# The opening of a fused attention and MLP kernel: triangles added by TensorE, v loaded whole by SyncE, quad 1 normalised in two parts, weight columns with stride two

## The chip, the cores and the metric

The kernel runs on one core of a Trainium2 chip. A core has a matmul engine (TensorE, PE in the profile; its weight loads are shown as PEld), VectorE (DVE), ScalarE (ACT), GpSimd (POOL) and SyncE (SP), each with its own queue of instructions, which it works through in order. They share the on-chip memory SBUF; matmuls write to PSUM, of which this kernel uses all eight banks. Loads and stores are issued by POOL (which can convert fp32 to bf16 on the way) and by SyncE, and are carried out by 16 DMA engines. The metric is the device time of one execution in microseconds; less is better. The profile's times count from the start of its span.

## The reference, cut to what matters

For 8 batches of 8 heads, 576 positions and 64 dimensions, a causal attention with a forget gate; its output, with the heads laid side by side to 512 columns, goes through a two-layer MLP with a tanh-approximated gelu and 2048 hidden columns.

```python
scores = scale * np.matmul(q, k.transpose(0, 1, 3, 2))
cum = np.cumsum(np.log(np.clip(f, 0.0001, 1.0)), axis=-1)
decay = cum[:, :, :, None] - cum[:, :, None, :]
scores = np.where(causal, -1000000000.0, scores + decay)
attn = np.exp(scores - np.max(scores, axis=-1, keepdims=True))
attn = attn / (np.sum(attn, axis=-1, keepdims=True) + 1e-09)
x = np.matmul(attn, v)            # then (batch, position, head * 64)
out = gelu_tanh(x @ w_in) @ w_out
```

The decay between a query and a key is a factor of the query times a factor of the key. The query's factor cancels in the division, so the kernel multiplies v, and the ones under the denominator, by the key's factor `wT`, and needs no decay on the scores.

## The kernel before

**Units of work.** Four heads of one batch are a quad; there are 16. A quad's scores are made with keys on the partitions and queries along the free axis, in three rounds (`rounds`): keys 0 to 127 against queries 0 to 511, then the last 64 queries of that strip with keys 128 to 255, then keys 256 to 511. The last 64 keys meet the last 64 queries in a corner of round 0 that would be masked anyway. In each round PE writes two pairs of PSUM banks (two heads each), ScalarE takes the exponential of each pair into `pt`, and POOL (`mask`, L182) writes zeros where the key is later than the query, with one `affine_select` per diagonal block, two for the first strip.

**From pt to xT.** `product` multiplies `pt` with a weight column. With `w_bf` it gives the denominators (`denominators`), with the weighted v, `vw`, the numerators, 32 dimensions of each head at a time (`out_groups(i, y)`). `reciprocals` transposes the denominators on VectorE (L220), inverts them (L222) and spreads them again (L224); `normalise` (L229) multiplies the numerators into `xT`, which is the MLP's input with the model dimension on the partitions. `make_vw` (L136) makes vw of a quad with two multiplies of 128x640 and two of 64x128 elements, the even and the odd dimensions of each head apart; it runs on VectorE for quads 0 and 1 and on POOL for the others.

**MLP.** `mlp_mm` (L241) multiplies 128 columns of w_in, the stationary operand, with 288 columns of xT; sixteen such column tiles make the hidden layer, each followed by a gelu on ScalarE (L250). `mlp_out` (L273) makes the output tiles from w_out, VectorE copies them out of PSUM (L278) and SyncE stores them. It is a generator: `pull` takes some of its matmuls at a time to fill PE's time between the attention rounds of the next quads.

**Order.** The order on each engine is the order in which the program writes it (`tc.manual_schedule()`). `startup` is the opening: it loads f, q and k of quads 0 and 1, v of batch 0 and the first half of w_in, makes the key factors, the transposed q and k (L125) and the vw of quads 0 and 1, and then interleaves the score rounds of both quads with their products. Some matmuls on a blank tile (`warm_up`, L297) are put in between. The rest of w_in (L115), q and k of quad 2, w_out (L119), q and k of quad 3 and v of batch 1 are loaded by POOL, between the masks. The main loop then runs, for batch 0, the hidden layer, `step(2)`, `step(3, 2)`, `step(4, 3)`: a step makes the scores of one quad and the products of the quad before it, in three rounds with fills. In these steps `make_vw(2)` stands in round 1 of its step and `make_vw(3)` and all later ones in round 0, between masks.

**Tiles.** Two bank pairs, tag "s", take turns for scores and hidden layer; one pair each has the tags "po" and "x". A product that is written to a pair waits until VectorE has read what stood there.

Of the kernel before, what the change touches and what calls it, by code (L numbers as in the profile page):

```python
# [16 lines left out]
def kernel(  # L17
# [67 lines left out]
    blank = singles.tile([128, 512], BF16, name="blank")  # L85
    pools = {"s": psS, "po": psO}
# [23 lines left out]
    w_out_hbm = moe_w_out.rearrange("(t p) n -> p t n", p=128)  # L110

    def load_w_in(c):
        n = slice(D_FF // 2 * c, D_FF // 2 * (c + 1))
        for u in range(QPB):
            nc.gpsimd.dma_start(out=w_in_sb[:, 2 * u:2 * u + 2, n], in_=w_in_hbm[u, :, :, n])  # L115

    def load_w_out(c):
        n = N_FT // 4
        return nc.gpsimd.dma_start(out=w_out_sb[:, n * c:n * (c + 1), :],  # L119
                            in_=w_out_hbm[:, n * c:n * (c + 1), :])  # L120
# [11 lines left out]
    def make_vw(i, eng=nc.gpsimd):  # L132
        h0 = 4 * (i % QPB)
        for p, n, slot in ((128, NT, 0), (64, 1, HEAD)):
            for y in range(2):
                eng.tensor_mul(  # L136
                    vw[i % 2][:p, slot:slot + n, :, 32 * y:32 * y + 32],
                    v_nat[(i // QPB) % 2][:p, 0:n, h0:h0 + 4, y::2],
                    wT[:p, i, 0:n, :].unsqueeze(3).to_broadcast([p, n, 4, D // 2]))
# [4 lines left out]
    def score_round(i, r, tags=("s", "s")):  # L144
# [19 lines left out]
        else:  # L164
            c0 = 0
            for (t, q0, nq) in parts:
                for c in range(2):
                    block(c, 0, 128, 128 * t, q0, nq, c0, c0 == 0)
                c0 += nq
        for g in range(2):  # L170
            nc.scalar.activation(p[:, 2 * g:2 * g + 2, off:off + n],  # L171
                                 tiles[g][:, :, 0:n], AF.Exp, scale=scale)

    def mask(i, r):
        p = pt[i % 2]
        for (t, q0, nq) in rounds[r][1]:
            if q0 == 128 * t:
                o = strip_off[t]
                within = [[0, 4], [1, 128]]
                for p0, p1, pattern in ([(0, 64, within), (64, 128, [[0, 4], [0, 2], [1, 64]])]  # L180
                                        if t == 0 else [(0, 128, within)]):
                    nc.gpsimd.affine_select(  # L182
                        out=p[p0:p1, :, o:o + 128], in_=p[p0:p1, :, o:o + 128],
                        compare_op=ALU.is_ge, fill=0.0, base=0, pattern=pattern,
# [33 lines left out]
    def reciprocals(i, po):  # L218
        den = den_pool.tile([128, S], FP32, name="den", tag="den")
        nc.vector.transpose(out=den, in_=po)  # L220
        rec = den_pool.tile([128, S // 32], FP32, name="rec", tag="rec")
        nc.vector.reciprocal(rec, den[:, 0:S:32])  # L222
        rb = den_pool.tile([128, S], FP32, name="rb", tag="rb")
        nc.vector.transpose(out=rb.rearrange("p (c j) -> p c j", j=32),  # L224
                            in_=rec.unsqueeze(2).to_broadcast([128, S // 32, 32]))
        rbs[i] = rb

    def normalise(i, y, po):
        nc.vector.tensor_mul(xT[i // QPB % 2][:, 2 * (i % QPB) + y, :], po, rbs[i])  # L229
# [7 lines left out]
    def mlp_mm(b, ft, ph, dts):  # L237
        hS = S // 2
        for dt in dts:
            for j in range(2):  # L240
                nc.tensor.matmul(  # L241
                    ph[:, j, 0:hS],
                    w_in_sb[:, dt, 128 * ft:128 * ft + 128],
# [55 lines left out]
    def startup():  # L299
        nc.sync.dma_start(out=f_sb, in_=f.rearrange("b h s -> (b h) s"))  # L300
        load_qk(0)
        make_identity(nc, ident_f32)
        load_qk(1)
        load_v(0, nc.gpsimd, slice(0, 4))
        load_v(0, nc.gpsimd, slice(4, 8))
        load_w_in(0)
# [27 lines left out]
        make_vw(1, nc.vector)  # L334

        for r, tags in enumerate((("s", "s"), ("x", "s"), ("s", "x"))):
            score_round(0, r, tags)
            warm_up(warm, 5)
            mask(0, r)
            if r == 0:  # L340
                load_w_in(1)
        score_round(1, 0)
        warm_up(warm, 5)
        score_round(1, 1, ("x", "s"))
        denominators(0)
        mask(1, 0)
        score_round(1, 2, ("s", "x"))
        attn_out(0, 0)
        mask(1, 1)
        load_qk(2)  # L350
        attn_out(0, 1, "s")
        mask(1, 2)
# [123 lines left out]
```

## Time and profile before

| | |
|---|---|
| median of 3 runs | 348.53 us (348.51 to 349.12) |
| the profiled execution, as a run | 348.87 us |
| its span | 347.2 us |
| PE busy | 334.9 us, 96% |
| ScalarE, VectorE, POOL busy | 198.4, 124.6, 131.5 us |
| matmuls of the hidden layer (L241) | 1024, 128.5 us |
| matmuls of the output layer (L273) | 1908, 134.6 us |
| POOL's selects (L182) | 80, 51.8 us |
| POOL's share of vw (L136) | 56 multiplies, 44.9 us |

A row of the timeline reads: start in us, duration in us, engine, line, operation, output and inputs, shape, how many instructions are merged into the row, and in brackets how long the engine stood idle before it and what ended that. A row by stretches gives the stretch, its length, and the busy time of PE, PEld, DVE, ACT and POOL, then the granted clock of TensorE, the busy share of the DMA engines and GB/s. A row of the DMA view gives a queue, its packets, MB and its share of 16 engines; q0 is POOL's queue, q1 SyncE's. A row of a group gives its busy time and the mean duration of one in ns, then the idle time before it.

### The profile page before, as it was taken

The page shows a single profiled execution, that of the slowest core. Times are in us where ns is not written, and L with a number is a line of the kernel's source. Part 1 is how long each engine was busy: PE and PEld are TensorE (multiplying, and loading weights), DVE is VectorE, ACT ScalarE, POOL GpSimd, SP SyncE. Part 2 cuts the span into 40 slices and gives each one's busy share as a digit, 9 for nine tenths or more (in the row PEclk, how much of TensorE's full clock was granted, in tenths as well). Part 3 has the DMA queues.
Part 4 walks back from the last instruction along what each step waited for, and adds up shares of the span by engine and source line. Part 5 has one row for each costly group of instructions (what it writes and reads, how often), then busy time and mean ns, then how long its engine had stood idle before and what let it go on. Part 6 is the DMA issues. An engine that isn't in the chain of part 4 may idle for free.

```text
span 347.2 us, 11023 instructions
## 1 busy us (share of the span) xinstructions
PE 334.9 (96%) x5022; PEld 197.6 (57%) x5022; DVE 124.6 (36%) x169; ACT 198.4 (57%) x244; POOL 131.5 (38%) x197
## 2 busy tenths in 40 slices
PE   7968999999999999999999999999999999999995
PEld 2336744477444774467554674457644675557642
DVE  7776034652342504433234413325133312430011
ACT  4853677676745567566655567566754566516400
POOL 8795339754162232716143241725035500200000
PEclk9989999999999999999999999999999999999999
DMA  7999998559311590019310391119201100010021
GB/s 127 202 180 207 220 188 198 98 89 229 61 62 64 112 192 32 34 59 206 70 65 35 102 203 31 37 60 186 50 34 63 51 14 2 35 62 30 2 89 63
DMA packets 42063, 33.37 MB, mean 96 GB/s; under 512 B 29600, under 2 KB 31648, under 8 KB 42016
## 3 DMA queue, kind: packets, MB, share of 16 engines
q0 software_dynamic: 8624, 15.99, 25.9%
q1 hardware_dynamic: 33392, 16.67, 17.3%
q8 instruction: 39, 0.64, 0.8%
q14 instruction: 8, 0.07, 0.1%
HBM read 36.85 MB, written 9.44 MB: 133 GB/s over the span
## 4 chain that ended last, share of the span: by engine, by line
PE 87%; ACT 5%; issue 2%; DMA 2%; POOL 2%; DVE 2%; ACTq 0%; DVEq 0%; POOLq 0%
PE ps_h L241 36%; PE pso L273 32%; PE po L198 10%; PE ps_s L151 8%; ACT pt L171 5%; DMA q_c<-in_q_dram 2%; POOL pt L182 1%; DVE den L220 0%; POOL w_in_sb L115 0%; DVE qT L125 0%; DVE rb L224 0%; DVE xT L229 0%; DVE o_st L278 0%; ACT gT L250 0%; POOL k_c L96 0%
## 5 line engine op out<-in xcount | busy, mean ns | idle before, releaser
L273 PE MATMUL pso<-w_out_sb,gT 128*32 128x512 bf16 (+1 forms) x1908 | 134.6, 379 | 0.0
L241 PE MATMUL ps_h<-xT,w_in_sb 128*128 128x288 bf16 x1024 | 128.5, 286 | 1.4 <-DVE xT L229 0.9
L171 ACT ACTIVATE pt<-ps_s 128x1024 bf16<-128x1024 f32 x96 | 92.6, 1024 | 51.7 <-PE ps_s L151 51.6
L250 ACT ACTIVATE gT<-ps_h 128x576 bf16<-128x576 f32 x128 | 82.5, 651 | 67.0 <-PE ps_h L241 67.0
L241 PEld LDWEIGHTS <-w_in_sb 128*128 128x128 bf16 x1024 | 99.5, 98 | 31.2 <-issue 5.1
L182 POOL TENSOR_SCALAR_AFFINE_SELECT pt<-pt 128x512 bf16<-128x512 bf16 (+1 forms) x80 | 51.8, 658 | 123.8 <-ACT pt L171 122.3
L273 PEld LDWEIGHTS <-gT 128*32 128x32 bf16 (+1 forms) x1908 | 59.0, 97 | 53.4 <-issue 0.8
L278 DVE COPY o_st<-pso 128x512 f32<-128x512 f32 x36 | 24.7, 685 | 71.0 <-PE pso L273 70.9
L136 POOL TENSOR_TENSOR vw<-v_nat,wT 128x640 bf16<-128x640 f32 (+1 forms) x56 | 44.9, 830 | 0.2
L220 DVE STREAM_TRANSPOSE den<-po 128x576 f32<-128x576 f32 x16 | 12.5, 783 | 83.8 <-PE po L198 83.8
L229 DVE TENSOR_TENSOR xT<-po,rb 128x576 bf16<-128x576 f32 x32 | 24.1, 757 | 46.3 <-PE po L198 46.1
L151 PE MATMUL ps_s<-qT,kT 32*64 32x64 bf16 (+6 forms) x896 | 35.9, 292 | 1.9 <-DVE qT L125 1.0
L151 PEld LDWEIGHTS <-kT 32*128 32x128 bf16 (+1 forms) x896 | 15.1, 97 | 27.4 <-issue 23.9
L198 PE MATMUL po<-pt,vw 128*32 128x64 bf16 (+4 forms) x768 | 28.8, 287 | 0.3 <-DVE den L220 0.3
L125 DVE STREAM_TRANSPOSE kT<-k_c 128x576 f32<-128x576 f32 x16 | 20.0, 1247 | 12.1 <-DMA k_c<-in_k_dram 12.1
L198 PEld LDWEIGHTS <-vw 128*32 128x32 bf16 x768 | 13.9, 99 | 14.8 <-issue 8.6
L96 POOL DMA_DIRECT2D k_c<-in_k_dram x16 | 9.2, 573 | 29.6 <-DVE kT L125 25.3
L125 DVE STREAM_TRANSPOSE qT<-q_c 128x576 f32<-128x576 f32 x16 | 19.9, 1243 | 1.1 <-DMA q_c<-in_q_dram 0.9
L198 PE MATMUL po<-pt,w_bf 128*32 128x512 bf16 (+5 forms) x384 | 15.2, 284 | 2.8 <-POOL pt L182 2.8
L102 POOL DMA_DIRECT2D v_nat<-in_v_dram x15 | 11.5, 775 | 8.2 <-DMA w_out_sb<-in_moe_w_out_dram 5.0
L224 DVE STREAM_TRANSPOSE rb<-rec 128x576 f32<-128x576 f32 x16 | 12.5, 778 | 0.5
L198 PEld LDWEIGHTS <-w_bf 128*1 128x1 bf16 (+1 forms) x384 | 6.5, 89 | 10.6 <-issue 6.1
(32 smaller groups left out, 69.2 us busy)
## 6 DMA issues: line engine op xcount, KB each, us to landing
out_dram<-o_st SPq DMA_DIRECT2D x36, 256.0 KB, 2.0
v_nat<-in_v_dram SPq DMA_DIRECT2D x24, 256.0 KB, 6.4
k_c<-in_k_dram POOLq DMA_DIRECT2D x16, 288.0 KB, 6.2
q_c<-in_q_dram POOLq DMA_DIRECT2D x16, 288.0 KB, 7.1
w_in_sb<-in_moe_w_in_dram POOLq DMA_DIRECT2D x4, 512.0 KB, 9.8
w_out_sb<-in_moe_w_out_dram POOLq DMA_DIRECT2D x4, 512.0 KB, 11.8
v_nat<-in_v_dram POOLq DMA_DIRECT2D x9, 128.0 KB, 7.3
v_nat<-in_v_dram POOLq DMA_DIRECT2D x4, 256.0 KB, 14.7
```

What stands on the lines that cost most here:

```text
L125: nc.vector.transpose(out=dst[i % 2].rearrange("p s c -> p (s c)").bitcast(FP32) .rearrange("p (t a) -> p a t", a=S // 32), in_=src[i % 2] ...
L136: eng.tensor_mul(vw[i % 2][:p, slot:slot + n, :, 32 * y:32 * y + 32], v_nat[(i // QPB) % 2][:p, 0:n, h0:h0 + 4, y::2], wT[:p, i, 0:n, :].u ...
L151: nc.tensor.matmul(tiles[h // 2][m0:m0 + m, h % 2, c0:c0 + nq], kk[32 * h:32 * h + 32, k0:k0 + m, c], qq[32 * h:32 * h + 32, q0:q0 + nq, c ...
L171: nc.scalar.activation(p[:, 2 * g:2 * g + 2, off:off + n], tiles[g][:, :, 0:n], AF.Exp, scale=scale)
L182: nc.gpsimd.affine_select(out=p[p0:p1, :, o:o + 128], in_=p[p0:p1, :, o:o + 128], compare_op=ALU.is_ge, fill=0.0, base=0, pattern=pattern, ...
L198: nc.tensor.matmul(po[r0:r0 + w.shape[-1], o:o + nq], w, p[:, h, col:col + nq], start=(n < 2), stop=(n in (0, len(product_parts) - 1)), sk ...
L220: nc.vector.transpose(out=den, in_=po)
L229: nc.vector.tensor_mul(xT[i // QPB % 2][:, 2 * (i % QPB) + y, :], po, rbs[i])
L241: nc.tensor.matmul(ph[:, j, 0:hS], w_in_sb[:, dt, 128 * ft:128 * ft + 128], xT[b % 2][:, dt, hS * j:hS * (j + 1)], start=(dt == 0), stop=( ...
L250: nc.scalar.activation(gT[:, ft, o:o + S].rearrange("p (j n) -> p j n", j=2), ph[:, :, 0:hS], AF.Gelu_apprx_tanh)
L273: nc.tensor.matmul(ps[m:m + w, :], gT[:, ft, c + m:c + m + w], w_out_sb[:, ft, :], start=(ft == 0), stop=(ft == N_FT - 1), skip_group_chec ...
L278: nc.vector.tensor_copy(st, ps)
```

## The change

**Masks of quads 0 and 1.** Two 128x128 tiles `lows` hold 0 where a key may be seen and -32768 elsewhere, one for the first strip with its folded corner and one for the other diagonal blocks. POOL makes them and a bf16 identity at the start. `score_round(..., masked=True)` adds the right one to each diagonal block of the scores with a matmul against the identity, so that the exponential gives zero; that is 16 matmuls of 128 columns for a quad. POOL's selects for these two quads are gone. Four of the groups of five warm-up matmuls become groups of four.

**Loads.** v of batch 0 is issued by SyncE in five whole tiles (eight heads), behind a wait for q of quad 0. The first load of w_in waits for the third of them. All of w_in, q and k of quad 2, w_out, q and k of quad 3, and v of batch 1 for its first four heads are issued by POOL one after the other; v of batch 1 for the other four heads is issued by SyncE once q of quad 3 is there. v of batch 2 is issued in step 2, after round 2.

**Quad 1.** `reciprocals` and `normalise` take a range of queries. After the products of the first four parts the queries 0 to 255 are complete; they are divided and written to xT, and the other 320 follow.

**Columns with stride two.** `make_vw` writes vw with the dimensions in order, in one multiply of 128x1280 and one of 64x256, and the product picks the even or odd ones with a stride of two. Likewise a hidden tile takes every second column of 256 columns of w_in, so that two neighbouring rows of w_out lie on one partition and are loaded as one run.

**Steps 2 and 3.** `make_vw(2)` and `make_vw(3)` move to the end of round 2 of their step, behind the last mask.

```diff
     w_in_hbm = moe_w_in.rearrange("(u p y) n -> u p y n", u=QPB, y=2)
-    w_out_hbm = moe_w_out.rearrange("(t p) n -> p t n", p=128)
+    w_out_hbm = moe_w_out.rearrange("(u p y) n -> p u y n", p=128, y=2)
...
     def make_vw(i, eng=nc.gpsimd):
         h0 = 4 * (i % QPB)
         for p, n, slot in ((128, NT, 0), (64, 1, HEAD)):
-            for y in range(2):
-                eng.tensor_mul(
-                    vw[i % 2][:p, slot:slot + n, :, 32 * y:32 * y + 32],
-                    v_nat[(i // QPB) % 2][:p, 0:n, h0:h0 + 4, y::2],
-                    wT[:p, i, 0:n, :].unsqueeze(3).to_broadcast([p, n, 4, D // 2]))
+            eng.tensor_mul(
+                vw[i % 2][:p, slot:slot + n], v_nat[(i // QPB) % 2][:p, 0:n, h0:h0 + 4, :],
+                wT[:p, i, 0:n, :].unsqueeze(3).to_broadcast([p, n, 4, D]))
...
+    def make_lows():
+        for low, parts in zip(lows, (diag_first, diag)):
+            nc.gpsimd.memset(low, 0.0)
+            for p0, p1, pattern in parts:
+                nc.gpsimd.affine_select(
+                    out=low[p0:p1, :], in_=low[p0:p1, :], compare_op=ALU.is_ge, fill=-32768.0,
+                    base=0, pattern=pattern, channel_multiplier=-1)
+
-    def score_round(i, r, tags=("s", "s")):
+    def score_round(i, r, tags=("s", "s"), masked=False):
...
+        if masked:
+            for g in range(2):
+                c0 = 0
+                for (t, q0, nq) in parts:
+                    for x in range(2 if q0 == 128 * t else 0):
+                        nc.tensor.matmul(tiles[g][:, x, c0:c0 + 128], ident, lows[t > 0],
+                                         start=False, stop=True, skip_group_check=True)
+                    c0 += nq
...
-        return [(32 * h, lambda t, h=h: vw[i % 2][:, t, h, 32 * y:32 * y + 32], h)
+        return [(32 * h, lambda t, h=h: vw[i % 2][:, t, h, y::2], h)
...
-                    w_in_sb[:, dt, 128 * ft:128 * ft + 128],
+                    w_in_sb[:, dt, 256 * (ft // 2) + ft % 2:256 * (ft // 2 + 1):2],
...
-        load_qk(0)
+        q0 = load_qk(0)[1]
         make_identity(nc, ident_f32)
         load_qk(1)
-        load_v(0, nc.gpsimd, slice(0, 4))
-        load_v(0, nc.gpsimd, slice(4, 8))
-        load_w_in(0)
+        v0 = load_v(0)
+        after(v0[0], q0)
+        make_identity(nc, ident)
+        make_lows()
...
         make_vw(0, nc.vector)
         make_vw(1, nc.vector)
+        after(load_w_in(0)[0], v0[2])
+        load_w_in(1)
+        load_qk(2)
+        for c in range(4):
+            load_w_out(c)
+        q3 = load_qk(3)[1]
+        load_v(1, nc.gpsimd, slice(0, 4))
+        after(load_v(1, heads=slice(4, 8))[0], q3)
...
-        first, rest = slice(0, 4), slice(4, 6)
+        first, rest, c = slice(0, 4), slice(4, 6), 256
         pod, po0, po1 = (bank_pair(x, "po") for x in ("s", "po", "x"))
-        product(1, den_groups(1), pod, first)
-        product(1, out_groups(1, 0), po0, first)
-        reciprocals(1, product(1, den_groups(1), pod, rest))
-        r0 = product(1, out_groups(1, 0), po0, rest)
-        r1 = product(1, out_groups(1, 1), po1)
+        reciprocals(1, product(1, den_groups(1), pod, first), 0, c)
+        for y, po in enumerate((po0, po1)):
+            normalise(1, y, product(1, out_groups(1, y), po, first), 0, c)
+        reciprocals(1, product(1, den_groups(1), pod, rest), c)
+        for y, po in enumerate((po0, po1)):
+            normalise(1, y, product(1, out_groups(1, y), po, rest), c)
...
-            if i is not None and r == (1 if i == 2 else 0):
+            if i is not None and r == 0 and i > 3:
                 make_vw(i)
             pull(fill, fills[r], 32)
             if i is not None and r == 2:
                 mask(i, 2)
-                if i in (3, 4):
+                if i < 4:
+                    make_vw(i)
+                if i == 2:
+                    load_v(2)
+                elif i < 5:
                     load_qk(i + 2)
```

More of the change, by code (lines that the diff above doesn't have):

```diff
@@ L85 @@
     blank = singles.tile([128, 512], BF16, name="blank")
+    ident = singles.tile([128, 128], BF16, name="ident")
+    lows = [singles.tile([128, 128], BF16, name=f"low{x}") for x in range(2)]
     pools = {"s": psS, "po": psO}
@@ L178, in mask @@
                 o = strip_off[t]
[L179 to L181 removed]
+                for p0, p1, pattern in (diag if t else diag_first):
                     nc.gpsimd.affine_select(
                         out=p[p0:p1, :, o:o + 128], in_=p[p0:p1, :, o:o + 128],
[L184 removed]
+                        compare_op=ALU.is_ge, fill=0.0, base=0, pattern=[[0, 4]] + pattern,
                         channel_multiplier=-1)
@@ L371, in startup @@
         gelu(0, 1, ph1)
-        load_qk(3)
-        after(load_v(2)[0], load_v(1, nc.gpsimd)[-1])
     def pull(it, n, cols=128):
```

61 lines of the change are left out of this document (29 added, 32 removed).

## The prediction

> **What bounds the kernel now.** I read the page first: the matmul engine is busy for 96% of the span, so only stretches where it isn't can be won.
>
> ```profile
> span 347.2 us, 11023 instructions
> PE 334.9 (96%) x5022; PEld 197.6 (57%) x5022; DVE 124.6 (36%) x169; ACT 198.4 (57%) x244; POOL 131.5 (38%) x197
> PEclk9989999999999999999999999999999999999999
> ```
>
> Then the table by stretches, cut where the granted clock changes. PE is busy 2.17 of 3.41 us, then 1.55, then works 3.41 us at a clock of 0.50.
>
> ```profile
> 15.24:18.65 3.41, 2.17 (x33) 0.76 (x33) 2.74 (x5) 3.41 (x5) 3.30 (x5) 1.00 1.02 129
> 18.65:22.06 3.41, 1.55 (x36) 0.74 (x39) 3.16 (x5) 0.78 (x2) 3.35 (x5) 1.00 1.02 172
> 22.06:25.47 3.41, 3.41 (x64) 2.04 (x67) 2.31 (x4) 2.87 (x3) 3.33 (x7) 0.50 1.12 211
> ```
>
> Last the timeline of the opening, up to the first matmuls that need quad 1 (29.22).
>
> ```profile
> 7.76 1.26 DVE L125 STREAM_TRANSPOSE qT<-q_c 128x576 f32<-128x576 f32 x1 [0.20 <-DMA q_c<-in_q_dram]
> 9.07 0.66 PE L151 MATMUL ps_s<-qT,kT 32*64 32x512 bf16 x24 [0.99 <-DVE qT L125]
> 9.67 1.25 PE L297 MATMUL warm<-blank 128*128 128x512 bf16 x5
> 9.82 9.27 ACT L171 ACTIVATE pt<-ps_s 128x1024 bf16<-128x1024 f32 x10 [2.31 <-PE ps_s L151]
> 11.04 1.26 DVE L125 STREAM_TRANSPOSE qT<-q_c 128x576 f32<-128x576 f32 x1 [0.34 <-DMA q_c<-in_q_dram]
> 13.99 3.01 DVE L136 TENSOR_TENSOR vw<-v_nat,wT 128x640 bf16<-128x640 f32 x4 [1.19 <-DMA v_nat<-in_v_dram]
> 17.68 3.27 DVE L136 TENSOR_TENSOR vw<-v_nat,wT 128x640 bf16<-128x640 f32 x4 [0.67 <-DMA v_nat<-in_v_dram]
> 19.05 0.36 PE L198 MATMUL po<-pt,w_bf 128*1 128x448 bf16 x4 [1.64 <-POOL pt L182]
> 20.22 0.31 PE L198 MATMUL po<-pt,w_bf 128*1 128x320 bf16 x4 [0.81 <-POOL pt L182]
> 21.16 0.78 DVE L220 STREAM_TRANSPOSE den<-po 128x576 f32<-128x576 f32 x1 [0.22 <-PE po L198]
> 23.54 0.76 DVE L229 TENSOR_TENSOR xT<-po,rb 128x576 bf16<-128x576 f32 x1 [0.49 <-PE po L198]
> 24.88 0.76 DVE L229 TENSOR_TENSOR xT<-po,rb 128x576 bf16<-128x576 f32 x1 [0.57 <-PE po L198]
> 26.41 0.78 DVE L220 STREAM_TRANSPOSE den<-po 128x576 f32<-128x576 f32 x1 [0.77 <-PE po L198]
> 28.41 1.42 DVE L229 TENSOR_TENSOR xT<-po,rb 128x576 bf16<-128x576 f32 x2
> 29.22 1.31 PE L241 MATMUL ps_h<-xT,w_in_sb 128*128 128x288 bf16 x8 [0.87 <-DVE xT L229]
> ```
>
> Two things end at 21: POOL's masks (PE waits 1.64 and 0.81 us for them) and VectorE's weighted v (17.68 + 3.27 = 20.95). Then VectorE's chain runs to 28.41 + 1.42 = 29.83, with 0.49 + 0.57 + 0.77 = 1.83 us of waits for a PE at half clock. From there the kernel is dense. So I sum over one number, the end of that chain, and then look for new waits.
>
> **The change part by part.** *Masks on TensorE.* 32 matmuls of 128 columns; a warm-up of 512 columns takes 1.25 / 5 = 0.25 us, so 0.06 each, 2.0 us, less four dropped warm-ups (1.0). A round costs PE 0.66 + 0.25 + 1.0 = 1.9 us, and ScalarE paces it with two exps of 0.93 (9.27 / 10): the first exp comes 0.1 later, the rest hides behind ScalarE; bare it would cost the 1.0. The seven small POOL instructions that build identity and triangles fall into 4 to 6 us, far ahead of 9.7. Both PE waits for masks go; the denominators of quad 0 run from about 17.4 (19.05 less the 1.64 of waiting) to 18.2. What is late next is vw on VectorE, so the masks alone would win next to nothing.
>
> *v by SyncE.* Ten half-tile loads leave POOL's queue; five whole ones go to SyncE's, behind a wait for q of quad 0 (7.76). Behind it on SyncE stands half of batch 1's v, which waits for q of quad 3 anyway. The load is 576 x 8 = 4608 packets of 256 B. How that queue fares is seen later in the span, alone and beside POOL's loads:
>
> ```profile
> DMA packets 1208, 0.31 MB, mean 218 GB/s; under 512 B 1208, under 2 KB 1208, under 8 KB 1208
> q1 hardware_dynamic: 1208, 0.31, 96.0%
> ...
> q0 software_dynamic: 259, 0.55, 94.8%
> q1 hardware_dynamic: 387, 0.10, 19.2%
> ...
> DMA to landing us min/median/max: 3.3/10.2/11.3
> ```
>
> The first two rows are 118.0 to 119.4 us, 863 packets per us; the next two 123 to 126, 129 per us beside POOL's 86. So from about 8.6 to 11.04 (q of quad 1 lands) 310 packets pass, and the other 4298 take 5.0 us: v is there at 16.0, with the landing 16.3. Ends: never slowed, 8.6 + 4608 / 863 = 13.9; as slow as the slowest tile in the third kind of row (one batch at 155 us), 8 + 11.3 = 19.3. I take 16.3: the contention ends at 11. Both quads' vw now wait for it, where quad 0's began at 13.99.
>
> *vw in one multiply.* Alone, a 128x640 multiply takes 0.82 us and a 64x128 one 0.27; beside POOL's selects the large one takes up to 1.41.
>
> ```profile
> 13.99 0.82 DVE L136 TENSOR_TENSOR vw<-v_nat,wT 128x640 bf16<-128x640 f32 x1 [1.19 <-DMA v_nat<-in_v_dram]
> ...
> L136 DVE TENSOR_TENSOR vw<-v_nat,wT x8: 274/780/1408, 14.0 to 20.2; 128x640 bf16<-128x640 f32 x4, 64x128 bf16<-64x128 f32 x4
> ```
>
> That is (0.82 - 0.27) / 512 = 1.07 ns an element. POOL now only issues loads in this time, so 1280 elements take 1.50 and 256 take 0.41; two quads 3.8, less three overlaps of some 0.07: 3.6 us against 3.01 + 3.27. vw ends at 19.9 instead of 20.95. Ends: 3.4 (no fixed part at all, 3072 x 1.07 = 3.3, and a start) and the old 6.3, if loads issued by POOL slowed it as selects do.
>
> *Quad 1 in two parts.* A quad's chain without waits is 26.41 to 29.83, 3.42 us. Quad 0 keeps 3.42. Of 0.78, some 0.18 is taken as fixed, the rest goes with columns: 256 columns save 0.33 on each of four instructions (2.1 us), 320 save 0.27 (2.3). The split alone thus adds 1.0 us of VectorE work (7.8 against 2 x 3.42); what pays is that PE's products (0.86 each at full clock, the row of 58.45 below) run under it. End: 19.9 + 7.8 = 27.7, against 29.83: **2.1 us won**.
>
> *The later steps.* vw of quads 2 and 3 moves on POOL behind all masks of its quad, and PE's products of those quads get a wait for POOL.
>
> ```profile
> 53.10 1.94 ACT L171 ACTIVATE pt<-ps_s 128x1024 bf16<-128x1024 f32 x2 [0.73 <-PE ps_s L151]
> 54.36 1.98 POOL L182 TENSOR_SCALAR_AFFINE_SELECT pt<-pt 128x512 bf16<-128x512 bf16 x3
> 56.31 3.20 POOL L136 TENSOR_TENSOR vw<-v_nat,wT 128x640 bf16<-128x640 f32 x4
> 58.45 0.86 PE L198 MATMUL po<-pt,vw 128*32 128x64 bf16 x24
> 63.29 1.23 POOL L182 TENSOR_SCALAR_AFFINE_SELECT pt<-pt 128x512 bf16<-128x512 bf16 x2 [1.76 <-ACT pt L171]
> 66.63 0.87 PE L198 MATMUL po<-pt,vw 128*32 128x64 bf16 x24
> 68.77 0.63 PE L151 MATMUL ps_s<-qT,kT 32*128 32x320 bf16 x14 [0.17 <-ACT pt L171]
> L182 POOL TENSOR_SCALAR_AFFINE_SELECT pt<-pt 128x512 bf16<-128x512 bf16 x48 | 30.6, 653 | 51.8 <-ACT pt L171 51.4
> ```
>
> Quad 2's masks end at 54.36 + 1.98 = 56.34. The four multiplies took 3.20; two of the same elements save two starts, about 0.15 each: 2.9. vw is ready at 59.2, and PE wants it at 58.45: PE, with all of the output projection queued behind, stands for 0.8 us. Quad 3: masks end at 64.52, vw at 67.4, wanted at 66.63: 0.8, of which some 0.3 comes back from PE's next wait for ScalarE (0.17 and the pause before). **1.3 us lost.** Ends: nothing, if the multiply ran at the select's 653 ns for 512 elements (1.6 + 0.4, ready at 58.3); 1.9 at the old 3.20. I take 2.9, the row of the same operation. The Trainium skill (GPSIMD Engine Reference, § 7) charges a POOL read more per element only when its step exceeds 8 bytes; the old step through v was just 8. By that page unit stride brings nothing here; no row before has that operation at unit stride.
>
> *Weight columns with stride two.* kT is already read so: its loads take no longer than those of w_in.
>
> ```profile
> L241 PEld LDWEIGHTS <-w_in_sb 128*128 128x128 bf16 x1024 | 99.5, 98 | 31.2 <-issue 5.1
> L151 PEld LDWEIGHTS <-kT 32*128 32x128 bf16 x512 | 9.2, 93 | 16.3 <-issue 15.0
> 31.02 13.88 PE ps_h L241 x112
> ```
>
> A matmul of the first layer comes every 13.88 / 112 = 124 ns and covers a load of 98: cost 0. Each ns beyond 124 would cost 1024 x 1 ns = 1.0 us.
>
> *Moved loads.* w_in waits on POOL for v's third tile; w_out, q and k of quads 2, 3 and v of batch 1 queue behind it without masks between. All of them are first used after 28 or, w_out and quads 2, 3, after the 13.88 us of dense matmuls: 0, though on that cover. Batch 2's v goes behind two output stores on SyncE, quad 5's q and k behind vw on POOL; both are used a block later: 0.
>
> **Sum:** -2.1 + 1.3 = -0.8 us on the profiled span of 347.2 us. That execution took 348.87 us as a run, 0.1% above the median of 348.53, so the difference is taken off the median: **347.7 us**. Own range 346.9 to 348.3, v 0.6 us earlier or later with the stalls between 1.1 and 1.5.
>
> **Rivals.** *v's tail meets w_in* (slower). w_in starts when three of v's five tiles are in; a DMA ring that lags then carries both. Against it: the other 1536 packets take only 1.8 us alone, and POOL must see the third tile land and issue before w_in moves. For it: 387 packets in 3 us beside POOL's loads, a landing of 10.2 us there, and in the opening itself vw of quad 1 waited for v until 17.68. At 129 instead of 863 per us, a fourth of that rest (384) takes 3.0 instead of 0.4: v at 19, vw 22.6, end 30.4, +0.6 + 1.3 = **350.4**. It decides from v at 17.1 on (17.1 + 11.4 = 28.5, where the gain is the 1.3 that the stalls take). The Trainium skill (DMA: Bandwidth & Descriptors, § Queues, rings and completion order) says that an engine alternates between its queues packet by packet, whatever their size: by that rule small packets always lose, as the 387 to 259 packets with 0.10 to 0.55 MB agree.
>
> *PE stays cold.* 1.55 of 3.41 us busy was followed by 0.50, 2.17 was not. After the change PE is busy in that stretch for some 0.7 + 1.2 = 1.9, between the two. Cold, two products of quad 0 take twice 0.86 and VectorE waits again, 0.49 as at 23.54: **348.2**, no change to measure.
>
> *The stall doesn't come* (POOL at its lower end) or v is there at 15: **346.4**.
>
> *Strided loads no longer hidden*: at twice 98, 72 ns x 1024 = +74 us; the kT row speaks against.
>
> **How the numbers follow.** Forecast 0.40, v's tail 0.28, cold PE 0.15, no stall or early v 0.15, loads 0.02. A measurement of this kernel tells about 0.2% (0.7 us) from no change. Faster: two thirds of the forecast, the no-stall case, a little of the cold one, 0.46; same 0.24; slower 0.30. Range 346.2 to 350.6, from just under the no-stall case to just over v's tail.
>
> **What would show it.** No PE wait for POOL before 30 us; vw multiplies starting at 16.3, four of them, the large ones near 1.5 us; the last xT ended by 27.7; two waits of PE for POOL's vw near 57 and 65; loads of w_in still 98 ns. Wrong if vw starts after 17.1, if PEclk shows 0.50 past 20, or if those two waits are absent.

## The result, and the profile after

The changed kernel takes 349.51 us (median of 20 runs, 348.69 to 352.75), the kernel before 348.49 us (20 runs, 347.61 to 349.29). The ratio is 1.0040, 95% interval 1.0024 to 1.0056: 0.4% slower (1.0 us between the medians, 1.4 us by the ratio), where the prediction had 0.8 us faster.

The head of the changed kernel's page answers to the first rows of the prediction. PE is busy 2.1 us longer than before (337.0 against 334.9), and the slice whose clock reads 8 tenths has moved one to the right.

```profile
span 347.9 us, 11049 instructions
PE 337.0 (97%) x5050; PEld 198.6 (57%) x5050; DVE 121.8 (35%) x170; ACT 198.8 (57%) x244; POOL 114.8 (33%) x156
PEclk9998999999999999999999999999999999999999
```

The timeline of its opening:

```profile
14.53 2.87 POOL L118 DMA_DIRECT2D w_in_sb<-in_moe_w_in_dram  x4 [7.31 <-DMA v_nat<-in_v_dram]
16.36 3.56 DVE L140 TENSOR_TENSOR vw<-v_nat,wT 128x1280 bf16<-128x1280 f32 x4 [4.22 <-DMA v_nat<-in_v_dram]
17.47 0.86 PE L218 MATMUL po<-pt,w_bf 128*32 128x64 bf16 x24
21.71 0.71 POOL L123 DMA_DIRECT2D w_out_sb<-in_moe_w_out_dram  x1 [1.81 <-DMA w_in_sb<-in_moe_w_in_dram]
24.40 0.72 POOL L123 DMA_DIRECT2D w_out_sb<-in_moe_w_out_dram  x1 [1.98 <-DMA w_in_sb<-in_moe_w_in_dram]
25.57 0.42 PE L263 MATMUL ps_h<-xT,w_in_sb 128*128 128x288 bf16 x2
26.50 0.89 DVE L250 TENSOR_TENSOR xT<-po,rb 128x320 bf16<-128x320 f32 x2
26.91 2.30 PE L263 MATMUL ps_h<-xT,w_in_sb 128*128 128x288 bf16 x10 [0.92 <-DMA w_in_sb<-in_moe_w_in_dram]
29.40 1.14 PE L263 MATMUL ps_h<-xT,w_in_sb 128*128 128x288 bf16 x4 [0.19 <-DMA w_in_sb<-in_moe_w_in_dram]
29.90 0.54 POOL L99 DMA_DIRECT2D q_c<-in_q_dram  x1 [1.93 <-DMA w_in_sb<-in_moe_w_in_dram]
30.80 3.47 PE L263 MATMUL ps_h<-xT,w_in_sb 128*128 128x288 bf16 x27 [0.26 <-ACT gT L272]
```

Down to VectorE the forecast came out: the multiplies start at 16.36, vw is done at 16.36 + 3.56 = 19.92, the denominators (17.47) wait for no mask, and the last xT ends at 26.50 + 0.89 = 27.39 instead of 29.83, 2.4 us earlier. Then nothing comes of it. The hidden layer runs two matmuls at 25.57 and stands; it goes on at 26.91 and again at 29.40, both times when a load of w_in lands. The dense part restarts at 30.80, where it did at 31.02 before. Which loads these are can be read from POOL: two of its issues of w_out wait for the first two loads of w_in, until 21.71 and 24.40. So 26.91 and 29.40 are the third and the fourth, the second half of w_in's columns, which the first hidden tiles don't multiply. The view of w_in's loads agrees: the longest takes 12.7 us from issue to landing, which for an issue at 16.7, the last of the four, gives 29.4.

By stretches, cut at the change of the clock, PE is busy 1.63 of 3.41 us in the waiting, and the next stretch runs at 0.50:

```profile
23.83:27.24 3.41, 1.63 (x29) 0.79 (x22) 3.10 (x9) 0.00 (x0) 0.72 (x1) 1.00 1.12 212
27.24:30.66 3.42, 3.11 (x13) 1.52 (x12) 0.15 (x1) 0.56 (x2) 1.10 (x2) 0.50 1.11 210
```

Later in the timeline stand the two waits for POOL's vw:

```profile
56.04 2.90 POOL L140 TENSOR_TENSOR vw<-v_nat,wT 128x1280 bf16<-128x1280 f32 x2
58.99 0.86 PE L218 MATMUL po<-pt,vw 128*32 128x64 bf16 x24 [0.77 <-POOL vw L140]
67.97 0.87 PE L218 MATMUL po<-pt,vw 128*32 128x64 bf16 x24 [0.74 <-POOL vw L140]
71.64 0.54 PE L263 MATMUL ps_h<-xT,w_in_sb 128*128 128x288 bf16 x3
```

The same point of the kernel before, the hidden layer of batch 1:

```profile
70.77 1.40 PE L241 MATMUL ps_h<-xT,w_in_sb 128*128 128x288 bf16 x10
```

So of 2.4 us won on VectorE, 0.2 are left at 30.8, and at 71.64 the changed kernel is 0.9 behind. Nearly the whole difference of these two executions is made by then (their spans differ by 0.7). The group of w_in's loads still has 98 ns:

```profile
L263 PEld LDWEIGHTS <-w_in_sb 128*128 128x128 bf16 x1024 | 99.9, 98 | 32.3 <-issue 3.7 <-DMA w_in_sb<-in_moe_w_in_dram 1.9
```

### The profile page after: what moved, and what is told of

Same layout as the page of the kernel before. It is cut to its first block, busy times and chain, and to the rows that moved or that the text cites. A ratio compares the mean times of both kernels' runs of the same rounds, so it can differ in the third digit from the quotient of the medians.

```text
span 347.9 us, 11049 instructions
## 1 busy us (share of the span) xinstructions
PE 337.0 (97%) x5050; PEld 198.6 (57%) x5050; DVE 121.8 (35%) x170; ACT 198.8 (57%) x244; POOL 114.8 (33%) x156
## 4 chain that ended last, share of the span: by engine, by line
PE 81%; DMA 7%; issue 5%; ACT 3%; POOL 3%; SPq 0%; DVE 0%; POOLq 0%; ACTq 0%
PE ps_h L263 36%; PE pso L295 31%; PE po L218 8%; PE ps_s L162 7%; DMA w_in_sb<-in_moe_w_in_dram 4%; ACT pt L190 3%; DMA v_nat<-in_v_dram 2%; DMA q_c<-in_q_dram 1%; POOL pt L202 1%; POOL vw L140 1%; POOL w_in_sb L118 0%; SPq L105 0%; DVE o_st L300 0%; ACT gT L272 0%; POOL k_c L99 0%
## 5 line engine op out<-in xcount | busy, mean ns | idle before, releaser
L263 PE MATMUL ps_h<-xT,w_in_sb 128*128 128x288 bf16 x1024 | 129.9, 288 | 1.4 <-DMA w_in_sb<-in_moe_w_in_dram 1.1
L202 POOL TENSOR_SCALAR_AFFINE_SELECT pt<-pt 128x512 bf16<-128x512 bf16 (+1 forms) x70 | 44.2, 641 | 128.9 <-ACT pt L190 127.8
L243 DVE STREAM_TRANSPOSE den<-po 128x576 f32<-128x576 f32 (+2 forms) x17 | 12.7, 746 | 80.9 <-PE po L218 80.9
L140 POOL TENSOR_TENSOR vw<-v_nat,wT 128x1280 bf16<-128x1280 f32 (+1 forms) x28 | 40.7, 1473 | 0.1
L250 DVE TENSOR_TENSOR xT<-po,rb 128x576 bf16<-128x576 f32 (+2 forms) x34 | 24.3, 721 | 46.6 <-PE po L218 46.3
L218 PE MATMUL po<-pt,vw 128*32 128x64 bf16 (+4 forms) x768 | 27.6, 279 | 3.3 <-POOL vw L140 1.5
L130 DVE STREAM_TRANSPOSE kT<-k_c 128x576 f32<-128x576 f32 x16 | 19.9, 1246 | 16.5 <-DMA k_c<-in_k_dram 16.5
L130 DVE STREAM_TRANSPOSE qT<-q_c 128x576 f32<-128x576 f32 x16 | 19.9, 1243 | 1.1 <-DMA q_c<-in_q_dram 1.1
L218 PE MATMUL po<-pt,w_bf 128*32 128x512 bf16 (+5 forms) x384 | 14.2, 279 | 0.0
L246 DVE STREAM_TRANSPOSE rb<-rec 128x576 f32<-128x576 f32 (+2 forms) x17 | 12.6, 743 | 0.6
L319 PE MATMUL warm<-blank 128*128 128x512 bf16 x33 | 10.4, 464 | 1.3 <-DVE blank L331 1.3
```

Of the source, the lines that this page charges most:

```text
L130: nc.vector.transpose(out=dst[i % 2].rearrange("p s c -> p (s c)").bitcast(FP32) .rearrange("p (t a) -> p a t", a=S // 32), in_=src[i % 2] ...
L140: eng.tensor_mul(vw[i % 2][:p, slot:slot + n], v_nat[(i // QPB) % 2][:p, 0:n, h0:h0 + 4, :], wT[:p, i, 0:n, :].unsqueeze(3).to_broadcast([ ...
L202: nc.gpsimd.affine_select(out=p[p0:p1, :, o:o + 128], in_=p[p0:p1, :, o:o + 128], compare_op=ALU.is_ge, fill=0.0, base=0, pattern=[[0, 4]] ...
L218: nc.tensor.matmul(po[r0:r0 + w.shape[-1], o:o + nq], w, p[:, h, col:col + nq], start=(n < 2), stop=(n in (0, len(product_parts) - 1)), sk ...
L243: nc.vector.transpose(out=den[:, c0:c1], in_=po[:, c0:c1])
L263: nc.tensor.matmul(ph[:, j, 0:hS], w_in_sb[:, dt, 256 * (ft // 2) + ft % 2:256 * (ft // 2 + 1):2], xT[b % 2][:, dt, hS * j:hS * (j + 1)], ...
```

## The experiments

All kernels were timed beside the kernel before on their own chip, so the ratios compare, not the medians; 0.001 is 0.35 us. "Restart" is where the dense hidden layer begins after the first gelu, in one profile each (30.80 above, 31.02 before). The base is the changed kernel with w_in in two tiles and with vw of quads 2 and 3 back at its old places.

| kernel | median us | before us | ratio (95%) | restart |
|---|---|---|---|---|
| changed kernel | 349.51 | 348.49 | 1.0040 (1.0024 to 1.0056) | 30.80 |
| w_in in two tiles | 347.19 | 348.11 | 0.9968 (0.9955 to 0.9980) | 28.38 |
| neighbouring columns | 347.55 | 348.11 | 0.9986 (0.9974 to 0.9998) | 28.30 |
| before + stride alone | 348.28 | 347.99 | 1.0009 (0.9996 to 1.0022) | 29.84 |
| steps back | 348.76 | 348.11 | 1.0015 (1.0001 to 1.0030) | 30.43 |
| base: two tiles, steps back | 346.44 | 348.11 | 0.9942 (0.9930 to 0.9954) | 28.16 |
| base, no split | 345.71 | 347.99 | 0.9933 (0.9918 to 0.9948) | 29.11 |
| base, POOL masks | 349.14 | 347.99 | 1.0035 (1.0022 to 1.0048) | 31.37 |
| base, v by POOL | 346.22 | 347.99 | 0.9947 (0.9934 to 0.9959) | 29.26 |
| base, no split, w_in behind all of v | 346.64 | 348.35 | 0.9949 (0.9937 to 0.9962) | 28.09 |
| base, no split, v at once | 345.66 | 348.35 | 0.9921 (0.9910 to 0.9933) | 28.12 |
| before + masks alone | 350.62 | 348.35 | 1.0059 (1.0042 to 1.0076) | 27.06 |
| before + masks + steps | 346.41 | 348.63 | 0.9937 (0.9921 to 0.9952) | 27.18 |
| base, no split, v in halves, first order | 353.07 | 348.63 | 1.0137 (1.0110 to 1.0164) | 36.76 |
| base, no split, v in halves | 344.88 | 348.00 | 0.9906 (0.9887 to 0.9925) | 27.35 |

### Who makes the hidden layer wait: two tiles, neighbouring columns, the stride alone

Theory: the strided slice of the one big tile `w_in_sb` is ordered behind a load that it doesn't read. The first rival is that w_in is late as a whole, the second that the half clock costs the time. First the tile is cut at the half of the columns:

```diff
-    w_in_sb = singles.tile([128, N_DT, D_FF], BF16, name="w_in_sb")
+    w_in_sb = many(2, [128, N_DT, D_FF // 2], BF16, "w_in_sb")
...
-                    w_in_sb[:, dt, 256 * (ft // 2) + ft % 2:256 * (ft // 2 + 1):2],
+                    w_in_sb[ft // 8][:, dt, 256 * (ft % 8 // 2) + ft % 2:256 * (ft % 8 // 2 + 1):2],
```

> The changed kernel with w_in held in two tiles, one for each half of its columns; stride, loads and their order stay. Theory (the first hidden tiles wait for the second half's loads because a strided slice of one big tile is ordered behind them; the loads land at 26.9 and 29.4 us): no wait for w_in is left before 30 us, the hidden layer runs on from 25.6 us, its dense part restarts at 28.6 to 29.6 instead of 30.8, and the time falls by 1.2 to 2.2 us, from 349.5 to about 347.8. Rival (w_in as a whole comes late, since all four loads now wait for v): the first half's loads are waited for too, restart within 0.3 us of 30.8, time 349.5. Rival (PE at half clock from 27.2 us is what costs): the waits go, the 0.50 stays, and the time falls by 0.5 us at most.

Then the big tile stays, with the columns and w_out's layout of the kernel before:

```diff
-                    w_in_sb[:, dt, 256 * (ft // 2) + ft % 2:256 * (ft // 2 + 1):2],
+                    w_in_sb[:, dt, 128 * ft:128 * ft + 128],
```

> The changed kernel with the weight columns of the kernel before: a hidden tile takes 128 neighbouring columns of w_in, and w_out lies as before. Theory (strided slices of one tile are ordered behind both halves): the same as with two tiles, no wait for w_in before 30 us and about 347.8 us (347.3 to 348.3). Rival (w_in late in any case): 349.5. If the stride itself cost time in the 1024 weight loads, this one would be faster than the one with two tiles; the theory expects the two within 0.3 us of each other.

And the reverse edit, with w_out's layout, in the kernel before:

> The kernel before with the strided weight columns alone (w_in's slice and the layout of w_out); loads, masks, v and steps stay. Its second half of w_in is issued at 16.6 us, eleven us before the first hidden tile. Theory (strided loads cost nothing, and the added order behind the second half costs only where that half is late): loads of w_in still 98 ns, the first tiles near 27.2 us with a wait of 0.3 us at most, and no difference to the kernel before (within 0.3 us). Rival (the stride costs by itself): 1024 loads, each ns past the cover 1 us, slower by more than 0.7 us; or a wait for w_in of 1 us or more near 28 us.

Timeline and stretches of the kernel with two tiles:

```profile
25.27 1.16 PE L263 MATMUL ps_h<-xT,w_in_sb 128*128 128x288 bf16 x8
26.21 0.89 DVE L250 TENSOR_TENSOR xT<-po,rb 128x320 bf16<-128x320 f32 x2
26.75 1.14 PE L263 MATMUL ps_h<-xT,w_in_sb 128*128 128x288 bf16 x8 [0.33 <-DVE xT L250]
28.38 3.35 PE L263 MATMUL ps_h<-xT,w_in_sb 128*128 128x288 bf16 x26 [0.49 <-ACT gT L272]
...
23.83:27.24 3.41, 2.31 (x29) 1.52 (x29) 2.99 (x8) 0.00 (x0) 0.72 (x1) 1.00 1.12 212
27.24:30.66 3.42, 2.93 (x25) 2.22 (x23) 0.00 (x0) 1.97 (x4) 1.10 (x2) 1.00 1.12 211
```

No wait for w_in is left, the clock stays at 1.00, and the restart is at 28.38. The time falls by 1.0040 - 0.9968 = 0.0072, 2.5 us, a little more than the 1.2 to 2.2 expected. With neighbouring columns the first hidden tiles run through as well:

```profile
25.18 1.15 PE L262 MATMUL ps_h<-xT,w_in_sb 128*128 128x288 bf16 x8
26.66 1.14 PE L262 MATMUL ps_h<-xT,w_in_sb 128*128 128x288 bf16 x8 [0.33 <-DVE xT L249]
```

In that profile POOL's issue of q still waits for w_in's last load until 29.93 (29.90 in the changed kernel), when these 16 matmuls have long ended: the load is as late as before, and is no longer waited for. The span is the same as with two tiles (345.4 against 345.5), but the runs spread more (347.01 to 349.52), and the ratio is 0.0018 higher, 0.6 us against the 0.3 expected at most, which stays unexplained. By this edit the wait costs 0.0054 or 1.9 us. In the kernel before, the stride alone changes nothing that can be measured (1.0009, interval over 1). So neither the stride nor the late loads cost by themselves; together they cost 1.9 to 2.5 us, by which edit takes the wait away. What makes the order is not shown. `w_in_sb` holds four blocks of model rows one behind the other on each partition, and one load fills half of the columns of two blocks. In the changed kernel the two matmuls of block 0 ran at 25.57, those of block 1 stood for the third load, those of block 2 ran, and the four of block 3 stood for the fourth. Taken as one range of addresses, from its first byte to its last, the third load holds the beginning of block 1 and the fourth that of block 3. A comparison of ranges thus fits these waits; but with neighbouring columns the same ranges hold the same blocks and nothing waits, so it would have to be made so coarsely for strided slices alone. No run tried this by itself.

### What the moved steps cost

```diff
-            if i is not None and r == 0 and i > 3:
+            if i is not None and r == (1 if i == 2 else 0):
                 make_vw(i)
...
-                if i < 4:
-                    make_vw(i)
```

> The changed kernel with vw of quads 2 and 3 made by POOL at the places of the kernel before (quad 2 after its second round, quad 3 at its first). Theory (two stalls of PE for vw, 0.77 and 0.74 us, of which a part comes back): both waits for POOL near 59 and 68 us go, the opening stays as it is, and the time falls by 0.9 to 1.5 us to about 348.3. Rival (what is won there is lost at the next wait for ScalarE): less than 0.4 us, 349.2 or more.

Both edits, two tiles and old steps, in one kernel:

> Two tiles for w_in and the steps of quads 2 and 3 at their old places, all else as in the changed kernel. Theory: the two effects add, 349.5 less 1.7 less 1.2, about 346.6 us (345.8 to 347.4), faster than both kernels by 0.3% or more. Rival (the opening's gain ends at another wait, such as PE's clock): 347.5 to 348.5, no better than the kernel before.

The two waits are gone in both kernels (below, 57.79 and 65.97 for the first). The time falls by 0.0025 and, with the tile cut, by 0.0026: 0.9 us, at the lower end of what was expected, and the two effects add. The rival that blames the half clock is settled here too: the kernel with the steps back has the same waits for w_in without the half clock, and restarts only 0.4 us earlier than the changed kernel:

```profile
27.02 1.40 PE L263 MATMUL ps_h<-xT,w_in_sb 128*128 128x288 bf16 x10 [0.34 <-DMA w_in_sb<-in_moe_w_in_dram]
29.28 0.67 PE L263 MATMUL ps_h<-xT,w_in_sb 128*128 128x288 bf16 x4 [0.85 <-DMA w_in_sb<-in_moe_w_in_dram]
30.43 1.75 PE L263 MATMUL ps_h<-xT,w_in_sb 128*128 128x288 bf16 x13 [0.49 <-ACT gT L272]
...
57.79 0.87 PE L218 MATMUL po<-pt,vw 128*32 128x64 bf16 x24
65.97 0.86 PE L218 MATMUL po<-pt,vw 128*32 128x64 bf16 x24
```

### What the parts of the opening are worth

All edits here start from the base. First quad 1 is normalised at once, with the lines of the kernel before in place of `reciprocals(1, ..., 0, c)` and those that follow:

> The version with two tiles and old steps (346.4 us where the kernel before takes 348.1), without quad 1's split: its 576 queries are normalised at once, in the order of the kernel before. By the prediction's step the split adds 1.0 us of VectorE work and pays because PE's products run under it. Unsplit, PE has the denominators at about 23.4, and a chain of 3.42 ends at 26.8 against 26.87 with the split: theory, no difference, 346.2 to 346.7. Rival (the split is what wins the opening): the last xT ends 0.5 to 2 us later, 346.9 to 348.4.

The multiplies of vw and the last xT, first with the split and then without it:

```profile
15.83 3.56 DVE L140 TENSOR_TENSOR vw<-v_nat,wT 128x1280 bf16<-128x1280 f32 x4 [3.55 <-DMA v_nat<-in_v_dram]
25.98 0.89 DVE L250 TENSOR_TENSOR xT<-po,rb 128x320 bf16<-128x320 f32 x2
```

```profile
17.30 3.56 DVE L140 TENSOR_TENSOR vw<-v_nat,wT 128x1280 bf16<-128x1280 f32 x4 [4.89 <-DMA v_nat<-in_v_dram]
26.49 1.42 DVE L250 TENSOR_TENSOR xT<-po,rb 128x576 bf16<-128x576 f32 x2
```

From the first multiply to the last xT it is 26.87 - 15.83 = 11.04 us with the split and 27.91 - 17.30 = 10.61 without. The split wins nothing: 0.9942 against 0.9933, and the intervals overlap. The loads are the same up to there, so the 1.5 us between the two starts are taken as scatter of v's landing.

Next the masks of quads 0 and 1 go back to POOL, with five warm-ups, w_in issued behind the first round's masks and POOL's other loads behind later ones:

```diff
-            score_round(0, r, tags, True)
-            warm_up(warm, 4)
+            score_round(0, r, tags)
+            warm_up(warm, 5)
+            mask(0, r)
+            if r == 0:
+                after(load_w_in(0)[0], v0[2])
+                load_w_in(1)
```

> The version with two tiles and old steps, with the masks of quads 0 and 1 back on POOL, five warm-ups a round, and POOL's loads between the masks at about the places of the kernel before (w_in, both halves, behind the first round's masks). v by SyncE, the single multiply and the split stay. Theory (masks and vw must both be early; POOL's selects slow VectorE's multiplies and hold the denominators): the multiplies of 3.56 us take 4 us or more, PE waits for masks by 0.5 to 1.7 us near 19 us, the last xT ends at 27.5 to 28.5 instead of 26.9, the time is 347.0 to 348.1. Rival (vw alone sets the opening): 346.4 within 0.3.

```profile
16.15 4.43 DVE L140 TENSOR_TENSOR vw<-v_nat,wT 128x1280 bf16<-128x1280 f32 x4 [3.35 <-DMA v_nat<-in_v_dram]
18.19 0.36 PE L218 MATMUL po<-pt,w_bf 128*1 128x448 bf16 x4 [1.21 <-POOL pt L202]
20.36 0.31 PE L218 MATMUL po<-pt,w_bf 128*1 128x320 bf16 x4 [1.81 <-POOL pt L202]
```

The multiplies take 4.43 us instead of 3.56, PE waits 1.21 and 1.81 us for masks, and after a stretch with PE busy for 1.14 of 3.41 us (18.48 to 21.89) the next one runs at 0.50, as in the kernel before. The time rises by 0.0093, 3.2 us, more than the 0.6 to 1.7 expected. No wait of PE for w_in stands there, so the moved issues of w_in don't explain it. v by POOL (`load_v(0, nc.gpsimd)`, no wait for q) changes nothing (0.9947 against 0.9942), though v lands at 16.94 in its profile; by the time the rival was right (whole tiles and the later w_in count, not the queue):

> The version with two tiles and old steps, with v's five whole tiles issued by POOL behind q and k of quad 1, and no wait for q of quad 0. Theory (SyncE's queue is what brings v early): v is there at 17.0 to 17.7 us, as in the kernel before, instead of 15.8, and the time is 347.4 to 348.1. Rival (whole tiles and the later w_in are what count, not the queue): v within 0.4 us of 15.8, and 346.4 within 0.3.

That leaves the masks on TensorE as what wins. They were then put into the kernel before, alone:

> The kernel before with one part of the change alone: the masks of quads 0 and 1 added by TensorE, four warm-ups a round, POOL's selects for these quads gone. v, vw, w_in, the weight columns, quad 1's order and the later steps stay as before. The prediction's step (vw on VectorE is late next, so the masks alone win next to nothing): time within 0.4 us of the kernel before. Theory after the run with masks on POOL, which took 2.7 us more: the selects also slow VectorE's multiplies (1.41 against 0.82 us) and leave PE idle enough for a stretch at half clock, so the masks alone win 1 to 2 us, 346.0 to 347.0; no clock of 0.50 before 30 us.

```profile
16.72 1.96 DVE L138 TENSOR_TENSOR vw<-v_nat,wT 128x640 bf16<-128x640 f32 x4 [1.91 <-DMA v_nat<-in_v_dram]
22.44 0.78 DVE L239 STREAM_TRANSPOSE den<-po 128x576 f32<-128x576 f32 x1 [0.39 <-PE po L217]
24.44 1.42 DVE L248 TENSOR_TENSOR xT<-po,rb 128x576 bf16<-128x576 f32 x2
27.06 4.69 PE L260 MATMUL ps_h<-xT,w_in_sb 128*128 128x288 bf16 x37 [0.49 <-ACT gT L269]
51.95 3.19 POOL L138 TENSOR_TENSOR vw<-v_nat,wT 128x640 bf16<-128x640 f32 x4 [4.84 <-DMA v_nat<-in_v_dram]
55.79 0.36 PE L217 MATMUL po<-pt,w_bf 128*1 128x448 bf16 x4 [3.66 <-POOL pt L201]
```

Both expectations missed the time: it is 0.6% slower. Yet the opening wins 4.0 us (27.06 against 31.02). Of these, 2.3 are there when vw is done, at 18.68 instead of 20.95: quad 1's four multiplies start at 16.72 instead of 17.68 and take 1.96 us instead of 3.27. The other 1.7 come behind it: the clock stays at 1.00 through the opening, VectorE's waits for PE shrink from 1.83 us to 0.39, and the last xT ends at 25.86. The gain turns into a new wait. Quad 2 now begins 4 us earlier, POOL stands 4.84 us ahead of its vw for v of batch 1, the masks queue behind it, and PE stands 3.66 us for them. PE is then busy for only 0.68 of the 3.41 us up to 56.98, and the next 3.41 us run at 0.50. If the place of vw is to blame, moving vw behind the masks, as the change does, must free the gain:

```diff
-            if i is not None and r == (1 if i == 2 else 0):
+            if i is not None and r == 0 and i > 3:
                 make_vw(i)
...
+                if i < 4:
+                    make_vw(i)
```

> The kernel before with the masks of quads 0 and 1 on TensorE, and vw of quads 2 and 3 behind all masks of their quads as in the changed kernel; nothing else. Theory (masks alone win 4 us in the opening, 27.06 against 31.02, and lose 4.2 us at 52 to 56 because POOL stands in vw of quad 2 for v of batch 1 with the masks queued behind): with vw behind the masks that wait holds no masks; PE waits for vw near 54 and 64 us by 0.7 to 1.0 each instead, and the time is 345.2 to 346.4 where the kernel before takes 348.2. Rival (the opening's gain isn't real end to end, later stages take it up wherever vw stands): 348 or more.

```profile
55.31 0.87 PE L217 MATMUL po<-pt,vw 128*32 128x64 bf16 x24 [0.70 <-POOL vw L138]
64.23 0.87 PE L217 MATMUL po<-pt,vw 128*32 128x64 bf16 x24 [0.68 <-POOL vw L138]
```

It does: 0.9937, 0.0122 or 4.3 us less than with the masks alone, with the two waits of 0.7 us and no stretch at 0.50. These two edits of the change, masks and steps, beat the whole change by 0.0103.

### v and w_in beside each other

The prediction's slower rival had v's tail meet w_in. `after(load_w_in(0)[0], v0[-1])` keeps them apart, in the kernel without split:

> The version with two tiles, old steps and no split (345.7 us), with w_in's first load behind v's last tile instead of its third, so that no w_in moves beside v. Rival of the prediction (v's tail meets w_in): the multiplies start at 15.5 us or before (third tile in at 14.5 and 1.0 for two more tiles), against 15.8 to 17.3 in six profiles of the same v; time lower by 0.3 to 1.2 us. Theory (the tail hardly meets w_in): start and time as before, 345.4 to 346.0.

```profile
16.14 3.56 DVE L140 TENSOR_TENSOR vw<-v_nat,wT 128x1280 bf16<-128x1280 f32 x4 [3.93 <-DMA v_nat<-in_v_dram]
26.45 1.16 PE L263 MATMUL ps_h<-xT,w_in_sb 128*128 128x288 bf16 x8 [1.17 <-DMA w_in_sb<-in_moe_w_in_dram]
```

v comes no earlier (16.14, within 15.8 to 17.3), and the later w_in is now waited for. So the rival falls at the size that it was given (v at 19, some 2.7 us late); an effect of less than the 1.5 us by which v's landing scatters would not show. Without the wait for q, v comes at 15.47, but the first exponential begins at 10.60 instead of 9.65; the time stays (0.9921 against 0.9933):

> The version with two tiles, old steps and no split (345.7 us), with v not waiting for q of quad 0. If v's start sets the opening: the multiplies start 0.5 to 1.5 us earlier and the time falls by as much. If q and v share the queues' time: q of quad 0 lands later than 7.4 us by 0.5 or more, the first exp with it, and the time is the same or higher, 345.7 to 346.7.

### The fastest version

With whole tiles quad 0's vw waits for the heads of quad 1. The last edit issues v of batch 0 in half tiles on POOL again, in the kernel without split. At first the triangles stood behind v's issues on POOL's queue, which the expectation had overlooked:

> The version with two tiles, old steps and no split (345.7 us where the kernel before takes 348.0), with v's ten half tiles issued by POOL as in the kernel before, w_in behind them with no wait. Theory (quad 0's multiplies needn't wait for the heads of quad 1: with masks alone they began at 12.87 and vw was complete at 18.7, against 19.4 to 20.9 with whole tiles): the denominators of quad 0 are read at 18.6, the dense hidden layer restarts near 27.1 instead of 28.1 to 29.1, the time is 0.7 to 1.5 us lower, 344.2 to 345.0. Rival (v's half tiles bring nothing, as the queue brought nothing): 345.4 to 346.0.

```profile
16.55 0.59 PE L186 MATMUL ps_s<-low,ident 128*128 128x128 bf16 x4 [7.16 <-POOL low L151]
```

PE waited 7.16 us for them, and its clock stood at 0.50 from 12.38 to 22.62. With the triangles first:

```diff
+        make_identity(nc, ident)
+        make_lows()
         load_v(0, nc.gpsimd, slice(0, 4))
         load_v(0, nc.gpsimd, slice(4, 8))
-        make_identity(nc, ident)
-        make_lows()
```

> As the version before it with v's ten half tiles issued by POOL, but with the identity and the triangles built ahead of those issues on POOL's queue (behind them PE waited 7.2 us for the triangles and the time was 353.1). Theory: no wait of PE for the triangles, quad 0's multiplies start near 12.9 and vw is complete near 18.7, the dense hidden layer restarts near 27.1 instead of 28.1 to 29.1, and the time is 344.2 to 345.2 where the kernel before takes 348.2. Rival (half tiles bring nothing): 345.4 to 346.2.

```profile
17.27 1.82 DVE L140 TENSOR_TENSOR vw<-v_nat,wT 128x1280 bf16<-128x1280 f32 x2 [2.45 <-DMA v_nat<-in_v_dram]
27.35 4.33 PE L263 MATMUL ps_h<-xT,w_in_sb 128*128 128x288 bf16 x34 [0.49 <-ACT gT L272]
```

It takes 344.88 us, ratio 0.9906 (0.9887 to 0.9925), 0.9% faster than the kernel before. Against whole tiles (0.9933, 0.9918 to 0.9948) the intervals still overlap, and the edit also moved v to POOL's queue and took away two waits, so what the half tiles alone are worth isn't shown.

## Why the prediction was wrong, by its own steps

- **Moved loads** and **weight columns with stride two**: these steps failed, each with the cost 0. The cover named for the loads, first use after 28 us, didn't hold: the first hidden tiles begin with the row blocks of quad 0, at 25.57 here and at 27.2 already in the kernel before. The first half of w_in was in by then, the second was not, and with the strided slice the third matmul of the first hidden tile waits for it. The wait costs 1.9 to 2.5 us and decides the sign. The loads themselves take 98 ns as said, and each edit alone costs nothing that was measured; the term that was missing belongs to the pair. Taken out, the kernel stands at 0.9968, 1.1 us faster than before, against the 0.8 of the sum.
- **v by SyncE, vw in one multiply**: start 16.36 for 16.3, multiplies 3.56 for 3.6, vw done at 19.92 for 19.9. The multiplies came out as reckoned. The hit on v's landing is luck in part, as it scatters by 1.5 us, and the queue, from which it was reckoned, brings nothing (v by POOL). With half tiles and the triangles first, vw was done at 17.27 + 1.82 = 19.09.
- **Masks on TensorE**: "the masks alone would win next to nothing" failed. They move the restart from 31.02 to 27.06, because without the selects VectorE's multiplies are faster (3.27 to 1.96 us) and the clock stays at 1.00 in the opening (VectorE's waits for PE fall from 1.83 to 0.39 us). The forecast put this gain down to v, to the single multiply and to the split. The masks alone still lose 0.6% in time, through the place of vw.
- **Quad 1 in two parts**: the added VectorE work was right in sign; that it pays was not, since 11.04 us against 10.61 without the split shows no gain.
- **The later steps**: multiplies of 2.90 for 2.9, waits of 0.77 and 0.74 for 0.8 and 0.5 net. The runs give 0.9 us for both instead of 1.3, so more came back at later waits than was taken. The price holds where v of batch 1 is early, as the change loads it; with the masks alone, where POOL stood for that v, the same move wins 4.3 us.
- **The rivals**: v's tail gave a loss of a similar size for a reason that the trace (multiplies at 16.36, not 19) and the run with w_in last speak against, so that it lay nearer to the result is luck. PE did run at half clock once, from 27.24, but after the wait for w_in, and by the run with the steps back it cost about 0.4 us.
- **The signs**: start and length of the multiplies, the last xT, the two later waits (2 to 3 us after their places) and the 98 ns came out as named, and only the clock spoke against the forecast. None of the signs looked at whether the first hidden tiles wait for w_in, the place where the gain was lost.

## What to carry to other kernels

When an edit changes how a tile is sliced and another delays the load of a part of it, read which loads the first use now waits for, part by part; a strided slice can be ordered behind a load whose data it doesn't touch, and here a tile for each half of the columns took that order away. Before moving work on an in-order queue, look at what stands behind it: vw ahead of the masks cost 4.3 us where the opening had won 4.0, and triangles behind v's issues cost 0.0231 or 8 us. A change of many parts is best timed part by part: here two of its edits win 0.6%, while all of them together lose 0.4%.

## What the runs showed of the hardware that was not expected

- **The clock.** A stretch with PE busy for 1.63 of 3.41 us was followed by one of 3.42 us at 0.50; with 2.31 us busy the clock stayed at 1.00. The Trainium skill (TensorE: Matmul & The Clock Gate, Part 1: The HAM clock gate) has the clock go back to half rate after an idle window of about 3.4 us. The length agrees; the condition doesn't, as this stretch was half busy. Apart from the last 10 us of a run, all sixteen profiles agree on a bound: the stretches at 1.00 with PE busy for 0.43, 0.68, 1.14, 1.21, 1.55 and 1.63 us were followed by 0.50, those with 1.92 us and more were not. It is no sure rule: at the end of the run without the split, a stretch with 1.47 us wasn't followed by 0.50.
- **POOL's multiply.** For the same elements two multiplies with unit stride take 2.90 us, four with a step of 8 bytes 3.19 to 3.20. The Trainium skill (GPSIMD Engine Reference, § 7) charges more only above 8 bytes; the 0.3 us left for two starts agree with that. From the means of the two sizes, the multiplies of 640 and 128 elements (1267 and 393 ns, step of 8 bytes) give 1.71 ns an element and 0.17 us a start, those of 1280 and 256 (2337 and 610 ns) 1.69 ns and 0.18 us.
- **v's landing scatters.** With the same loads up to there (the changed kernel, the two tiles, the neighbouring columns, the steps back, the base and the base without split) the multiplies began between 15.83 and 17.30 us, so one profile of an opening tells less than its ratio over runs.
